# Block attention and an ELU feed-forward on one core: the first stage and the first chunk in a fixed order on all engines

## The chip, the cores and the metric

One core of a Trainium2 chip. A core has five engines that each work through a queue of their own, in order: TensorE (PE in the profile, its weight loads PEld), VectorE (DVE), ScalarE (ACT), GpSimd (POOL) and SyncE (SP), which here only issues DMAs. They wait for each other by semaphores. The time is the device time of one execution in microseconds (us); the profile gives a span, from the first to the last instruction, for one profiled execution.

## The reference

Attention over 4 batches, 8 heads, 768 positions, 64 dimensions, where each query sees its window of 31 neighbours and 24 block summaries (maxima of k, means of v, blocks of 32); its output goes through a feed-forward with an ELU.

```python
k_sum = k.reshape(B, H, nb, block, D).max(axis=3)
v_sum = v.reshape(B, H, nb, block, D).mean(axis=3)
scores_l = scale * np.matmul(q, k.transpose(0, 1, 3, 2))
mask_l = np.abs(pos[:, None] - pos[None, :]) < window
scores_s = scale * np.einsum('bhsd,bhnd->bhsn', q, k_sum) + np.log(block)
scores_all = np.concatenate([np.where(mask_l, scores_l, -1e9), scores_s], axis=-1)
a = np.exp(scores_all - np.max(scores_all, axis=-1, keepdims=True))
a = a / (np.sum(a, axis=-1, keepdims=True) + 1e-09)
attn = np.matmul(a, np.concatenate([v, v_sum], axis=2))
...
h = x @ w_in                       # x: (3072, 512), w_in: (512, 2048)
g = np.where(h > 0.0, h, np.exp(np.minimum(h, 0.0)) - 1.0)
out = g @ w_out                    # w_out: (2048, 512)
```

## The kernel before

Heads go in pairs (`NP` = 4), so that a pair fills 128 partitions. Positions go in thirds of a batch, 256 each, split into four query blocks of 64; a block's keys are the 96 positions around it and the 24 summaries, 120 columns (`KC`). One third of one pair is a *unit*: scores, the lows (`softmax` begins with the negated score's minimum per row, one VectorE instruction per block), four exponentials on ACT with their row sums `z`, a reciprocal on VectorE, a normalization on POOL, four transposes, a copy to `pt`, eight value products, and `take_x`, which splits the output into a rounded high part `xh` (ACT) and a rest `xl` (VectorE).

Two thirds make a *chunk* of 512 tokens; there are six. The feed-forward of a chunk has 16 *slots* `f`: `layer1` is twelve products (high and low parts of x and w) into `h`, then the exponential (ACT, L415), min and max (VectorE, L416 and L417), the high part `gh` (ACT, L420) and the rest `gl` (POOL, L421); `layer2` of the slot before is twelve products into four banks. Between the two stands a piece of unit work: in even slots the scores of a coming unit and the transposes of the current one, in odd slots its value products. In chunk 0 scores, transposes and value products share one bank, `a0`.

The weights come as raw 64-bit words, 32 pieces of 128x512, and each is converted once, in chunk 0 or just ahead of it (`convert`). The steps are called here *mul* (ACT, L96, into the bank `sh`), *lo* (POOL, L98, in place), *sh* and *cv* (VectorE, L100 and L103), *copy* (ACT, L106, the high part) and *sub* (POOL, L107, the rest).

`first_units` does the first two thirds of batch 0 for all four pairs: it loads `kn`, copies its bands and maxima into `k_t`, puts q into block-diagonal tiles `q_t`, sums v by blocks on TensorE (`vsps`), and puts the means into the value tiles. `load_unit` loads q, k and v of a later unit, `summary` the maxima and sums of the next batch.

Order: within `first_units` only SP's queue is written out by hand; in the loop over slots SP's and TensorE's are. All other queues are ordered by a scheduler that goes by costs of its own, led by a few marks (`issue_after`) that hold an instruction until another has been placed. SP's queue has the loads of the first ten weights ahead of the first units' q, k and v; from then on three weights a slot.

Of the kernel before, what the change touches and what calls it, by code (L numbers as in the profile page):

```python
# [26 lines left out]
P = 128  # L27
# [11 lines left out]
def attn_elu_ffn(ctx: ExitStack, tc: tile.TileContext, qT, kT, vT, v, w_in, w_out, out):  # L39
# [32 lines left out]
    raws, weights = {}, {}  # L72

# [12 lines left out]
    def convert(key, turn):  # L86

        raw = raws.pop(key)
        lo_w, hi_w = raw[:, :, 0], raw[:, :, 1]
        sh = psum.tile([P, WC], F32, tag="a1", name="sh")
        bits = sh.bitcast(U32)
        with tc.issue_after(turn[1]):
            nc.scalar.mul(out=sh, in_=hi_w.bitcast(F32), mul=2.0 ** -112)  # L96
        with tc.issue_after(turn[2]):
            nc.gpsimd.tensor_scalar(out=lo_w, in0=lo_w.bitcast(U8)[:, :, 3], scalar1=1 / 32, scalar2=-31 / 64,  # L98
                                    op0=ALU.mult, op1=ALU.add)
        nc.vector.scalar_tensor_tensor(out=bits, in0=bits, scalar=3, in1=lo_w,  # L100
                                       op0=ALU.logical_shift_left, op1=ALU.bitwise_or)
        cv = ffn.tile([P, WC], F32, tag="cv", name="cv", bufs=2)
        nc.vector.scalar_tensor_tensor(out=cv.bitcast(U32), in0=hi_w, scalar=0x80000000, in1=bits,  # L103
                                       op0=ALU.bitwise_and, op1=ALU.bitwise_or)
        w = wts.tile([P, 2, WC], F32R, tag=f"w{key[0]}_{key[1]}", name=f"w{key[0]}_{key[1]}")
        nc.scalar.copy(out=w[:, 0, :], in_=cv)  # L106
        nc.gpsimd.tensor_tensor(out=w[:, 1, :], in0=cv, in1=w[:, 0, :].bitcast(F32), op=ALU.subtract)  # L107
        weights[key] = w
# [4 lines left out]
    def softmax(th, s_ps, sm):  # L113
        mx = att.tile([P, UW, 1], F32, tag="mx", name="mx", bufs=4)
        for t in range(UW):
            w = th * UW + t
            m = mask[:, 0 if w == 0 else 2 if w == NTH * UW - 1 else 1, :]
            low = nc.vector.tensor_tensor_reduce(out=sm[:, t, :], in0=s_ps[:, t, :], in1=m, scale=-scale, scalar=3.0e38,  # L118
                                           op0=ALU.add, op1=ALU.min, accum_out=mx[:, t, :])
        z = att.tile([P, UW, 1], F32, tag="z", name="z", bufs=4)  # L120
        for t in range(UW):
            exp = nc.scalar.activation(out=sm[:, t, :], in_=sm[:, t, :], func=AF.Exp, bias=mx[:, t, :], scale=-1.0,  # L122
                                 accum_out=z[:, t, :])
        nc.vector.tensor_scalar(out=z, in0=z, scalar1=1e-9, scalar2=None, op0=ALU.add)
        nc.vector.reciprocal(out=z, in_=z)
        mul = nc.gpsimd.tensor_tensor(out=sm, in0=sm, in1=z.broadcast_to([P, UW, KC]), op=ALU.mult)  # L126
        return low.ins, exp.ins, mul.ins
# [27 lines left out]
    def put_means(b, p, v_t, copy=None):  # L155
        n = v_t.shape[1]
        src = vs_all[b][KB:KC, p * P:(p + 1) * P].rearrange("n (o d) -> n o d", o=1).broadcast_to([NS, n, P])
# [11 lines left out]
    def first_units():  # L169


        new_x(0)
# [5 lines left out]
        def borrow(shape, name):  # L178
            return wts.tile(shape, F32, tag=free.pop(0), name=name)
# [3 lines left out]
        pt_tags = free[:NP]  # L183
        q_t = [borrow([P, W2, P], f"q{p}") for p in range(NP)]
        sm_tags = free[:NP]
        kn = [borrow([P, E + S], f"kn{p}") for p in range(NP)]
        k_t = [borrow([P, W2, KC], f"k{p}") for p in range(NP)]
        vn = [borrow([P, 2, row], f"vn{j}") for j in range(NTH)]
        mean = borrow([P, 2 * BLK], "mean")
        qn = borrow([P, 2, CH], "qn")  # L190
        sms, pts = {}, {}

        for h in range(2):
# [5 lines left out]
            masked = nc.gpsimd.affine_select(out=m[:, 0:KB], in_=m[:, 0:KB], compare_op=ALU.is_ge, fill=NEG / scale,  # L201
# [17 lines left out]
        for _ in range(2):
            nc.tensor.matmul(idle_ps, zero[:, 0:P], zero, start=True, stop=True)  # L220
        for p in range(NP):
            nc.vector.memset(kn[p][:, 0:E], 0.0)
            for h in range(2 if p < 2 else 0):
                nc.vector.memset(q_t[p][h * D:(h + 1) * D, :, (1 - h) * D:(2 - h) * D], 0.0)

        def load_kn(p):
            nc.sync.dma_start(out=kn[p][:, E:E + S], in_=kT[0, p])

        def load_q(p):
            for h in range(2):  # L230
# [12 lines left out]
        for key in order[:2]:
            load(key)
# [6 lines left out]
        for key in order[2:10]:  # L251
            load(key)

        warm = const.tile([P, 1], F32, name="warm")
        nc.vector.memset(warm, 0.0)
        nc.scalar.activation(out=warm, in_=warm, func=AF.Exp)
        with tc.issue_after(masked.ins):

            per = P // BLK
            nc.gpsimd.memset(mean, 0.0)  # L260
            for r in range(per):
                nc.gpsimd.memset(mean[r * BLK:(r + 1) * BLK, BLK + r:BLK + r + 1], 1.0 / BLK)
            for i in range(2):
                nc.gpsimd.memset(qbd[i], 0.0)
            for p in range(NP):
                nc.gpsimd.memset(kw[p][:, UW - 1, KB - E:KB], 0.0)
                nc.gpsimd.memset(vw[p][QW:KB, UW - 1, :], 0.0)

        ends = []
        for p in range(NP):  # L270
            if p < 2:
                for h in range(2):
                    nc.scalar.copy(out=q_t[p][h * D:(h + 1) * D, :, h * D:(h + 1) * D],
                                   in_=qn[h * D:(h + 1) * D, p].rearrange("d (t q) -> d t q", q=QW))
            band = bass.AP(tensor=kn[p].tensor, offset=kn[p].offset, ap=[list(kn[p].ap[0]), [QW, W2], [1, KB]])
            with tc.issue_after(ends[p - 1][0]) if p > 0 else ExitStack():
                nc.vector.tensor_reduce(out=ks[:, p, :], in_=kn[p][:, E:E + S].rearrange("p (n k) -> p n k", k=BLK),
                                        axis=AX.X, op=ALU.max)
                if p == 0:
                    nc.vector.tensor_copy(out=k_t[p][:, :, 0:KB], in_=band)  # L280
# [262 lines left out]
```

## Time and profile before

| what | value |
|---|---|
| time, median of 3 runs | 677.4 us (676.89 to 679.43) |
| profiled execution: time, span | 677.08 us, 675.3 us |
| mean granted TensorE clock | 0.987 |
| TensorE busy | 651.6 us, 96% of the span |
| VectorE, ScalarE, GpSimd busy | 275.1, 279.9, 248.8 us |
| DMA | 60.21 MB; 28.5% of the engines' time on SP's queue |
| load sizes, KB each | kn 384 (x4), vn 512 (x3), raw weight 512 (x32), v 336 and 40 (x4 each), qn 256 |

Rows of a timeline read: start in us from the span's start, length in us, engine, line, operation, output and inputs by the program's names, sizes, count; in brackets the idle time before it and what ended it. One fp32 product shows as two records, so eight products appear as x16; L412 and L432 use a rounded type with one record each. Rows of a group read: line, engine, operation, sizes, count, then busy us and mean ns of one, then idle time before. In the rows of stretches the columns are start and end, length, busy time (and count) of PE, PEld, DVE, ACT and POOL, granted clock as a share of full speed, mean busy share of the DMA engines, GB/s.

### The profile page before, as it was taken

To read this page: it belongs to the slowest core of one execution; us is meant where nothing else is said; L and a number is where in the kernel's file an instruction comes from. 1 tells how busy PE (TensorE), PEld (TensorE's weight loads), DVE (VectorE), ACT (ScalarE), POOL (GpSimd) and SP (SyncE) were. 2 spreads that over 40 slices of the span, in tenths; PEclk is the share of its full clock that TensorE was granted. 3 is DMA by queue.
4 is the path that set the end of the run, shared out by engine and by line. 5 is a ranking of instruction groups with operands and counts; after the bars stand their busy time and mean duration, and the time that the engine had idled before them with its cause. 6 is when DMAs were issued, how large, how long until landed. Compare 5 with 4: busy or idle time off the path is not lost.

```text
span 675.3 us, 10292 instructions
## 1 busy us (share of the span) xinstructions
PE 651.6 (96%) x3688; PEld 530.0 (78%) x3688; DVE 275.1 (41%) x866; ACT 279.9 (41%) x753; POOL 248.8 (37%) x269
## 2 busy tenths in 40 slices
PE   7879899999999999999999999999999999999996
PEld 4557777888888888888888888888888888888884
DVE  6677986773333543222322553232332222211122
ACT  5465666674333334433433533343443333322221
POOL 7466787983223222322322232222223222222221
PEclk9779999999999999999999999999999999999999
DMA  9969992113112341411212443121312100100001
GB/s 297 298 189 320 323 292 70 35 42 99 47 32 80 98 131 42 125 32 32 61 33 54 139 127 85 38 53 44 94 35 57 32 1 1 63 0 1 0 1 63
DMA packets 88002, 60.21 MB, mean 89 GB/s; under 512 B 48528, under 2 KB 80272, under 8 KB 87952
## 3 DMA queue, kind: packets, MB, share of 16 engines
q1 hardware_dynamic: 84208, 52.74, 28.5%
q10 hardware_dynamic: 3744, 6.82, 2.7%
q8 instruction: 29, 0.48, 0.3%
q14 instruction: 21, 0.17, 0.1%
HBM read 52.46 MB, written 6.29 MB: 87 GB/s over the span
## 4 chain that ended last, share of the span: by engine, by line
PE 84%; DMA 6%; DVE 2%; POOL 2%; SPq 2%; ACT 1%; issue 1%; POOLq 0%; DVEq 0%; ACTq 0%
PE h L412 37%; PE o L432 36%; PE s L386 5%; PE o_ps L139 3%; PE t_ps L132 2%; DMA raw_w<-in_w_out_dram 2%; DMA raw_w<-in_w_in_dram 1%; DMA v<-in_v_dram 1%; DMA n<-in_kT_dram 1%; DMA vw<-in_v_dram 1%; POOL w L107 1%; SPq L158 1%; PE s L289 1%; POOL raw_w L98 1%; POOL gl L421 1%
## 5 line engine op out<-in xcount | busy, mean ns | idle before, releaser
L412 PE MATMUL h<-xh,w 128*128 128x512 f32 x768 | 262.1, 402 | 1.5 <-ACT xh L152 1.5
L421 POOL TENSOR_TENSOR gl<-e,gh 128x512 fp32r<-128x512 f32 x96 | 123.4, 1286 | 206.7 <-issue 114.3
L432 PE MATMUL o<-w,gh 128*128 128x512 f32 x768 | 196.3, 394 | 0.0
L412 PEld LDWEIGHTS h<-xh,w 128*128 128x128 f32 x768 | 144.5, 188 | 33.4 <-ACT xh L152 1.6
L432 PEld LDWEIGHTS o<-w,gh 128*128 128x128 f32 x768 | 141.3, 188 | 27.5 <-ACT gh L420 0.3
L416 DVE TENSOR_SCALAR e<-e 128x512 f32<-128x512 f32 x96 | 49.3, 513 | 260.6 <-ACT e L415 260.5
L412 PE MATMUL h<-xl,w 128*128 128x512 f32 x384 | 150.3, 392 | 0.2 <-DVE xl L153 0.2
L415 ACT ACTIVATE e<-h 128x512 f32<-128x512 f32 x96 | 57.2, 596 | 205.2 <-PE h L412 205.2
L126 POOL TENSOR_TENSOR sm<-sm,z 128x480 f32<-128x480 f32 x48 | 48.1, 1002 | 162.1 <-ACT gh L420 136.7
L432 PE MATMUL o<-w,gl 128*128 128x512 f32 x384 | 105.8, 390 | 0.7 <-POOL gl L421 0.7
L420 ACT CAST gh<-e 128x512 fp32r<-128x512 f32 x96 | 58.9, 614 | 67.4 <-DVE e L417 66.1
L122 ACT ACTIVATE sm<-sm,mx 128x120 f32<-128x120 f32 x192 | 73.6, 384 | 31.2 <-DVE mx L118 28.5
L432 PEld LDWEIGHTS o<-w,gl 128*128 128x128 f32 x384 | 72.1, 188 | 16.2 <-POOL gl L421 1.1
L412 PEld LDWEIGHTS h<-xl,w 128*128 128x128 f32 x384 | 72.5, 189 | 13.3 <-DVE xl L153 0.6
L417 DVE SCALAR_TENSOR_TENSOR e<-h,e 128x512 f32<-128x512 f32 x96 | 66.1, 688 | 1.9
L386 PEld LDWEIGHTS s<-kw,qbd 128*128 128x128 f32 x320 | 42.5, 194 | 5.1 <-DVE xl L153 2.1
L107 POOL TENSOR_TENSOR w<-cv,w 128x512 fp32r<-128x512 f32 x32 | 42.0, 1318 | 11.7 <-ACT w L106 11.1
L386 PE MATMUL s<-kw,qbd 128*128 128x120 f32 x320 | 43.0, 278 | 1.7 <-DVE xl L153 1.7
L118 DVE CUSTOM_DVE_ANT_0 sm<-s,mask 128x120 f32<-128x120 f32 x192 | 42.5, 276 | 4.5 <-PE s L289 3.3
L153 DVE TENSOR_TENSOR xl<-o_ps,xh 128x256 fp32r<-128x256 f32 x48 | 20.0, 421 | 56.8 <-ACT xh L152 56.7
L122 ACT ACTIVATION_READ_ACCUMULATOR sm<-sm,mx 128x1 f32 x192 | 35.9, 187 | 0.0
L133 ACT COPY pt<-t_ps 120x512 f32<-120x512 f32 x44 | 25.6, 583 | 22.8 <-PE t_ps L132 22.4
(65 smaller groups left out, 394.5 us busy)
## 6 DMA issues: line engine op xcount, KB each, us to landing
raw_w<-in_w_in_dram SPq DMA_DIRECT2D x16, 512.0 KB, 6.4
raw_w<-in_w_out_dram SPq DMA_DIRECT2D x16, 512.0 KB, 8.2
out_dram<-ot ACTq DMA_DIRECT2D x24, 256.0 KB, 3.4
qbd<-in_qT_dram SPq DMA_DIRECT2D x80, 64.0 KB, 2.4
kw<-in_kT_dram SPq DMA_DIRECT2D x28, 144.0 KB
vw<-in_v_dram SPq DMA_DIRECT2D x28, 144.0 KB, 3.8
n<-in_kT_dram SPq DMA_DIRECT2D x16, 192.0 KB, 2.6
n<-in_vT_dram SPq DMA_DIRECT2D x16, 192.0 KB, 2.4
```

Source lines behind the costliest of these rows:

```text
L107: nc.gpsimd.tensor_tensor(out=w[:, 1, :], in0=cv, in1=w[:, 0, :].bitcast(F32), op=ALU.subtract)
L118: low = nc.vector.tensor_tensor_reduce(out=sm[:, t, :], in0=s_ps[:, t, :], in1=m, scale=-scale, scalar=3.0e38, op0=ALU.add, op1=ALU.min, a ...
L122: exp = nc.scalar.activation(out=sm[:, t, :], in_=sm[:, t, :], func=AF.Exp, bias=mx[:, t, :], scale=-1.0, accum_out=z[:, t, :])
L126: mul = nc.gpsimd.tensor_tensor(out=sm, in0=sm, in1=z.broadcast_to([P, UW, KC]), op=ALU.mult)
L386: nc.tensor.matmul(s_ps[:, t, :], qbd[u % 2][:, t, :], kw[p][:, t, :], start=True, stop=True)
L412: nc.tensor.matmul(h_ps, w[:, a, cols], bb[:, cc, :], start=(k == 0), stop=(k == 3 * NCC - 1))
L415: exp = nc.scalar.activation(out=e, in_=h_ps, func=AF.Exp)
L416: nc.vector.tensor_scalar(out=e, in0=e, scalar1=1.0, scalar2=-1.0, op0=ALU.min, op1=ALU.add)
L417: elu = nc.vector.scalar_tensor_tensor(out=e, in0=h_ps, scalar=0.0, in1=e, op0=ALU.max, op1=ALU.add)
L420: nc.scalar.copy(out=gh, in_=e)
L421: low = nc.gpsimd.tensor_tensor(out=gl, in0=e, in1=gh.bitcast(F32), op=ALU.subtract)
L432: nc.tensor.matmul(o_acc[c][s], a[:, s * P:(s + 1) * P], w[:, bb, :], start=first and f == 0, stop=last and f == NF - 1)
```

## The change

The whole first stage and the sixteen slots of chunk 0 are written in a fixed order for all five engines; the scheduler keeps VectorE, ScalarE and GpSimd from chunk 1 on. In the first stage scores are formed straight from `kn` and `qn` as loaded, each head by itself on its 64 rows of the array into its 64 partitions of the bank, first all windows (96 columns), then all summaries (24 columns); the tiles `k_t` and `q_t` go. Means for two of the four value tiles are copied from the bank of the sums, not from `vs`. The value sums move on TensorE behind all scores and the first pair's transposes. Weights are loaded and converted in the order (1,0), (1,1), (2,0), (1,2), (2,1) and so on; three are converted ahead of slot 0 and two in each slot, one of them wholly ahead of the slot's exponential. SP loads one weight ahead of v, two behind it, then units and weights by turns.

```diff
+    order = [(1, 0)]
+    for f in range(1, NF):
+        order += [(1, f), (2, f - 1)]
+    order.append((2, NF - 1))
...
-    def convert(key, turn):
+    def convert(tag="a1"):
+        key = todo.pop(0)
...
-        with tc.issue_after(turn[1]):
-            nc.scalar.mul(out=sh, in_=hi_w.bitcast(F32), mul=2.0 ** -112)
-        with tc.issue_after(turn[2]):
-            nc.gpsimd.tensor_scalar(out=lo_w, in0=lo_w.bitcast(U8)[:, :, 3], scalar1=1 / 32, scalar2=-31 / 64,
-                                    op0=ALU.mult, op1=ALU.add)
+        nc.scalar.mul(out=sh, in_=hi_w.bitcast(F32), mul=2.0 ** -112)
+        nc.gpsimd.tensor_scalar(out=lo_w, in0=lo_w.bitcast(U8)[:, :, 3], scalar1=1 / 32, scalar2=-31 / 64,
+                                op0=ALU.mult, op1=ALU.add)
+        yield
         nc.vector.scalar_tensor_tensor(out=bits, in0=bits, scalar=3, in1=lo_w,
                                        op0=ALU.logical_shift_left, op1=ALU.bitwise_or)
...
+        yield
         w = wts.tile([P, 2, WC], F32R, tag=f"w{key[0]}_{key[1]}", name=f"w{key[0]}_{key[1]}")
...
+        def scores(p):
+            q_p = qn[p // 2][:, p % 2]
...
+            for cols in (slice(0, KB), slice(KB, KC)):
+                for th in range(2):
+                    for t in range(UW):
+                        w = th * UW + t
+                        for h in range(2):
+                            rows = slice(h * D, (h + 1) * D)
+                            right = kn[p][rows, w * QW:w * QW + KB] if cols.start == 0 else ks[rows, p, :]
+                            nc.tensor.matmul(banks_of[p, th][rows, t, cols], q_p[rows, w * QW:(w + 1) * QW], right,
+                                             start=True, stop=True)
...
+        put_means(0, 0, v_t[0], act, ps)
+        put_means(0, 1, v_t[1], dve, ps)
+        act(out=vs[KB:KC], in_=ps[KB:KC])
+        one = convert(tag="o3")
+        next(one)
+        put_means(0, 2, v_t[2], pool)
+        put_means(0, 3, v_t[3], pool)
...
+    with tc.manual_schedule(engines=set(engines.values())):
+        first_units()
+        got = {}
+        for n in range(NF):
+            u, odd = divmod(n, 2)
+            h_ps = layer1(0, n)
+            one = convert() if todo else iter(())
+            list(one)
+            if not odd:
+                unit_scores(u + 1, 0)
+                load_unit(u + 2)
...
+            load_more(12 + 3 * (n + 1))
+            e, _ = elu(0, n, h_ps)
+            two = convert() if todo else iter(())
+            next(two, None)
+            split(0, n, e)
+            if not odd:
+                low = unit_low(u + 1)
+                next(two, None)
+                unit_exps(u + 1, low)
+            else:
+                unit_norm(u + 1)
+            list(two)
+            if n > 0:
+                layer2(0, n - 1)
...
+            slot_b(n, 0)
+
+    with tc.manual_schedule(engines={engines["PE"], engines["SP"]}):
+        for n in range(NF, NCH * NF):
```

How the built program's queues read, at three places. GpSimd's queue in chunk 0, from one `gl` to the next (raw_w and w are one weight before and after its conversion, the numbers its slot and the buffer). Before:

```order
L421 TENSOR_TENSOR gl<-e,gh 128x512
L98 TENSOR_SCALAR raw_w_6_690<-raw_w_6_690 128x512
L98 TENSOR_SCALAR raw_w_6_692<-raw_w_6_692 128x512
L107 TENSOR_TENSOR w_5_874<-cv,w_5_874 128x512
L161 COPY kw_75<-ks 128x4x24
L107 TENSOR_TENSOR w_5_883<-cv,w_5_883 128x512
```

GpSimd's queue in slot 2 and the beginning of slot 3, after the change:

```order
L106 TENSOR_SCALAR raw_w_4_203<-raw_w_4_203 128x512
L117 TENSOR_TENSOR w_4_848<-cv,w_4_848 128x512
L106 TENSOR_SCALAR raw_w_3_205<-raw_w_3_205 128x512
L510 TENSOR_TENSOR gl<-e,gh 128x512
L117 TENSOR_TENSOR w_3_897<-cv,w_3_897 128x512
L106 TENSOR_SCALAR raw_w_5_661<-raw_w_5_661 128x512
L117 TENSOR_TENSOR w_5_940<-cv,w_5_940 128x512
```

Before, both lo of the next slot's weights stand ahead of the subs of this slot's; after, each weight's lo and sub follow each other, with the next weight's lo behind them.

ScalarE's queue in chunk 0 over about one and a half slots, before:

```order
L106 CAST w_4_788<-cv 128x512
L96 ACTIVATE sh<-raw_w_5_550 128x512
L420 CAST gh<-e 128x512
L152 CAST xh<-o_ps 128x256
L106 CAST w_5_874<-cv 128x512
L96 ACTIVATE sh<-raw_w_5_552 128x512
L415 ACTIVATE e<-h 128x512
L106 CAST w_5_883<-cv 128x512
L96 ACTIVATE sh<-raw_w_6_690 128x512
L122 ACTIVATE sm,z<-sm,mx 128x120 x4
L420 CAST gh<-e 128x512
```

ScalarE's queue in slot 2 and the beginning of slot 3, after:

```order
L105 ACTIVATE sh<-raw_w_4_203 128x512
L116 CAST w_4_848<-cv 128x512
L501 ACTIVATE e<-h 128x512
L105 ACTIVATE sh<-raw_w_3_205 128x512
L509 CAST gh<-e 128x512
L136 ACTIVATE sm,z<-sm,mx 128x120 x4
L116 CAST w_3_897<-cv 128x512
L149 COPY pt<-t_ps 120x512
L105 ACTIVATE sh<-raw_w_5_661 128x512
L116 CAST w_5_940<-cv 128x512
```

Before, a mul follows right behind the copy of the weight ahead of it, with other work between it and its own copy; after, the first weight's mul and copy are neighbours and the exponential stands behind them.

TensorE's queue in the first stage, from the first scores on (sm, pt and v end in the number of a pair's buffer), before:

```order
L289 MATMUL s<-k_100,q_92 128x120 x8
L289 MATMUL s<-k_101,q_93 128x120 x8
L298 MATMUL vsps<-vn_104,mean 32x512 x2
L298 MATMUL vsps<-vn_105,mean 32x512 x2
L298 MATMUL vsps<-vn_106,mean 32x512 x2
L132 MATMUL t_ps<-ident,sm_219 120x128 x8
L289 MATMUL s<-k_102,q_94 128x120 x8
L132 MATMUL t_ps<-ident,sm_262 120x128 x4
L289 MATMUL s<-k_103,q_95 128x120 x8
```

And after:

```order
L287 MATMUL s<-kn_98,qn_96 64x96 x16
L287 MATMUL s<-ks,qn_96 64x24 x16
L287 MATMUL s<-kn_99,qn_96 64x96 x16
L287 MATMUL s<-ks,qn_96 64x24 x16
L287 MATMUL s<-kn_100,qn_97 64x96 x16
L287 MATMUL s<-ks,qn_97 64x24 x16
L287 MATMUL s<-kn_101,qn_97 64x96 x16
L287 MATMUL s<-ks,qn_97 64x24 x16
L148 MATMUL t_ps<-ident,sm_243 120x128 x8
L309 MATMUL vsps<-vn_92,mean 32x512 x2
```

The value sums stood between the second and the third pair's scores and stand behind all four pairs' and the first transposes now; each pair's eight products of 120 columns are 32 of 96 and 24.

More of the change, by code (lines that the diff above doesn't have):

```diff
@@ L301, in first_units @@
[L301 to L309 removed]
+        load_more(3)
@@ new lines, in vals, with sums @@
+        def vals(p, th):
+            take_x(values(v_t[p], th * UW, pts[p][:, th], ("a0", "o0", "o1", "o2")[2 * (p % 2) + th]), th, p)
+        def sums(j0, j1):
+            for j in range(j0, j1):
+                nc.tensor.matmul(ps[KB:KB + BLK, :], mean[:, BLK - per * j:2 * BLK - per * j],
+                                 vn[j // 2][:, j % 2, :], start=(j == 0), stop=(j == 2 * NTH - 1),
+                                 tile_position=(0, KB))
+        dve, act, pool = nc.vector.tensor_copy, nc.scalar.copy, nc.gpsimd.tensor_copy
@@ new lines, in first_units @@
+        ps = psum.tile([P, row], F32, tag="a1", name="vsps")
+        sums(0, 2 * NTH)
+        norm(3, 0)
+        trans(1, 0, act)
+        trans(1, 1, dve)
+        norm(3, 1)
+        put_means(0, 0, v_t[0], act, ps)
[5 more added lines that the diff above has]
+        put_means(0, 3, v_t[3], pool)
+        trans(2, 0, act)
+        vals(0, 0)
+        trans(2, 1, dve)
@@ L310, in first_units @@
+        vals(0, 1)
+        next(one)
+        trans(3, 0, act)
+        vals(1, 0)
+        trans(3, 1, dve)
+        list(one)
+        vals(1, 1)
+        two = convert()
+        next(two)
+        vals(2, 0)
+        vals(2, 1)
+        next(two)
+        vals(3, 0)
+        vals(3, 1)
         for p in range(NP):
             put_maxima(0, p)
-        return ends[2]
+        unit_scores(0, 0)
+        low = unit_low(0)
+        list(two)
+        three = convert(tag="o3")
+        next(three)
@@ L315, in attn_elu_ffn @@
+        unit_exps(0, low)
+        next(three)
+        unit_norm(0)
+        list(three)
+        for p in range(NP):
+            put_means(0, p, vw[p])
+        load_more(12)
     units = [(third, p) for third in range(2, NTH * B) for p in range(NP)]
@@ L472, in attn_elu_ffn, with slot_b @@
-    convert_more(6, end)
-    first_of = {th // NTH: 4 * (th - 2) for th in range(NTH, NTH * B, NTH)}
-    unit_scores(0, 0)
-    with tc.manual_schedule(engines={mybir.EngineType.PE, mybir.EngineType.SP}):
-        for n in range(NCH * NF):
+    first_of = {th // NTH: 4 * (th - 2) for th in range(NTH, NTH * B, NTH)}
+    def slot_b(n, c):
+        u, odd = divmod(n, 2)
+        if u < len(units):
+            (unit_values if odd else unit_transposes)(u, c)
+        for b, first in first_of.items():
+            if n == 2 * first - 2:
+                means(b, c)
+            p, late = divmod(n - (2 * first - 1), 2)
+            if 0 <= p < NP and not late:
+                put_means(b, p, vw[p])
```

307 lines of the change are left out of this document (150 added, 157 removed).

## The prediction

> **What bounds the kernel now.** I read the page's head, then the busy times of three stretches, and last the timelines of TensorE, ScalarE, VectorE and GpSimd over the first 160 us.
>
> ```profile
> span 675.3 us, 10292 instructions
> ...
> PE 651.6 (96%) x3688; PEld 530.0 (78%) x3688; DVE 275.1 (41%) x866; ACT 279.9 (41%) x753; POOL 248.8 (37%) x269
> ```
> ```profile
> 0.00:45.95 45.95, 34.62 (x233) 25.57 (x233) 31.80 (x124) 25.15 (x88) 29.18 (x64) 0.87 0.95 265
> 45.95:157.95 112.00, 106.04 (x622) 85.33 (x621) 83.58 (x196) 71.66 (x178) 84.82 (x85) 0.99 0.60 176
> 157.95:675.30 517.35, 510.94 (x2840) 419.15 (x2836) 159.69 (x547) 183.12 (x487) 134.83 (x121) 1.00 0.20 55
> ```
> ```profile
> 45.95 0.77 PE L412 MATMUL h<-xh,w 128*128 128x512 f32 x1
> ...
> 54.83 0.48 PE L412 MATMUL h<-xh,w 128*128 128x512 f32 x1
> ...
> 118.69 0.50 PE L412 MATMUL h<-xh,w 128*128 128x512 f32 x1
> ...
> 157.95 0.50 PE L412 MATMUL h<-xh,w 128*128 128x512 f32 x1
> ```
>
> The second fence's columns are stretch, length, and busy time of PE, PEld, DVE, ACT and POOL, then clock, DMA share and GB/s. Three stages show: the first stage until the first layer-1 product (45.95), the sixteen slots of chunk 0 (until 157.95), and the rest, where TensorE idles 6 of 517 us. At the chunk's end six slots take 157.95 - 118.69 = 39.26 us, 13.09 a pair, which is TensorE's own work there; later slots keep that pace, and the change leaves their order as it was. All the change can do lies before 157.95. Sixteen slots at that pace, less one missing layer 2 (12 products of about 0.23, 2.7 us), would take 102; they take 112. So 10 us of stall in chunk 0 and the length of the first stage are what can be won.
>
> **Part 1: one pass of the new slot.** In chunk 0 each slot converts two weights, the first wholly (mul, lo, sh, cv, copy, sub) ahead of the exponential, the second spread behind it. Queues run in order, so the pass closes on itself: ACT's second copy releases POOL's sub, behind that stands the next slot's lo, for which DVE's sh waits, then cv, ACT's copy, behind that the exponential, DVE's min and max, behind them the lows, sh and cv of the second weight, and its copy. Before, POOL did both lo ahead of the subs, and ACT issued the next mul right behind each copy. Its links, from rows:
>
> ```profile
> 57.87 0.60 ACT L415 ACTIVATE e<-h 128x512 f32<-128x512 f32 x1 [1.32 <-PE h L412]
> 60.16 0.62 ACT L420 CAST gh<-e 128x512 fp32r<-128x512 f32 x1 [1.70 <-DVE e L417]
> ...
> 63.77 0.63 ACT L96 ACTIVATE sh<-raw_w 128x512 f32<-128x512 f32 x1
> ...
> 66.02 0.62 ACT L106 CAST w<-cv 128x512 fp32r<-128x512 f32 x1 [1.11 <-DVE cv L103]
> 66.55 0.63 ACT L96 ACTIVATE sh<-raw_w 128x512 f32<-128x512 f32 x1
> ```
> ```profile
> 49.47 0.17 DVE L124 TENSOR_SCALAR z<-z 128x4 f32<-128x4 f32 x1
> 49.67 0.18 DVE L125 RECIPROCAL z<-z 128x4 f32<-128x4 f32 x1
> ...
> 54.22 0.42 DVE L416 TENSOR_SCALAR e<-e 128x512 f32<-128x512 f32 x1
> ...
> 58.50 0.91 DVE L416 TENSOR_SCALAR e<-e 128x512 f32<-128x512 f32 x1 [1.76 <-ACT e L415]
> 59.44 0.69 DVE L417 SCALAR_TENSOR_TENSOR e<-h,e 128x512 f32<-128x512 f32 x1
> ...
> 64.49 0.70 DVE L100 SCALAR_TENSOR_TENSOR sh<-sh,raw_w 128x512 uint32<-128x512 uint32 x1 [1.02 <-ACT sh L96]
> 65.22 0.69 DVE L103 SCALAR_TENSOR_TENSOR cv<-raw_w,sh 128x512 uint32<-128x512 uint32 x1
> ...
> 81.58 0.27 DVE L118 CUSTOM_DVE_ANT_0 sm<-s,mask 128x120 f32<-128x120 f32 x1
> ...
> 82.39 0.68 DVE L417 SCALAR_TENSOR_TENSOR e<-h,e 128x512 f32<-128x512 f32 x1
> 83.00 0.68 DVE L100 SCALAR_TENSOR_TENSOR sh<-sh,raw_w 128x512 uint32<-128x512 uint32 x1
> ```
> ```profile
> 57.84 1.29 POOL L421 TENSOR_TENSOR gl<-e,gh 128x512 fp32r<-128x512 f32 x1
> 59.21 1.44 POOL L98 TENSOR_SCALAR raw_w<-raw_w 128x512 uint32<-128x512 uint8 x2
> 60.87 1.28 POOL L421 TENSOR_TENSOR gl<-e,gh 128x512 fp32r<-128x512 f32 x1 [0.22 <-ACT gh L420]
> ...
> 66.72 1.29 POOL L107 TENSOR_TENSOR w<-cv,w 128x512 fp32r<-128x512 f32 x1 [1.49 <-ACT w L106]
> ```
> ```profile
> L126 POOL TENSOR_TENSOR sm<-sm,z 128x480 f32<-128x480 f32 x13 | 13.5, 1041 | 11.1 <-ACT sm L122 8.0 <-DVE z L125 2.6
> ```
>
> Copy to sub 66.72 - 66.02 = 0.70. Sub to lo 1.37 (GpSimd's 57.84 to 59.21, same size). Lo to sh 0.75 (1.44 for two, back to back about 0.66 each, and 0.09 as from mul's end at 64.40 to 64.49). Sh to cv 0.73, cv to copy 0.80. From the copy on, the exponential starts after 0.53 (66.02 to 66.55) and ends 0.60 later, but min does not take its free 0.42 (54.22, where GpSimd was idle): at 58.50 it ran beside a GpSimd subtraction that ended at 59.13 and itself ended at 59.41, 0.28 later. Here the first weight's sub starts 0.70 after the copy and lasts 1.29, always across min: min ends 0.70 + 1.29 + 0.28 = 2.27 after the copy (1.58 if it never met it, my lower end). Min to the step behind max 0.03 + 0.61 (82.39 to 83.00). Then in an even slot four lows, 0.81 (81.58 to 82.39), in an odd one z and its reciprocal, 0.3. Sh, cv, copy again 1.53. Odd: 0.70 + 1.37 + 0.75 + 1.53 + 2.27 + 0.64 + 0.3 + 1.53 = 9.1. Even: 0.81 instead of 0.3 gives 9.6, and 0.5 more, since the odd slot's gl and the unit's normalization (1.28 and 1.04) stand on POOL ahead of its last sub: 10.1. A pair takes 19.2, where TensorE's work takes 13.1: chunk 0 goes at the pace of the three small engines. TensorE cannot run ahead: the unit's scores and its transposes share one bank, so transposes wait for the lows of their own slot. What TensorE wants from these engines otherwise (gh, gl, xh, weights two slots ahead) is there in time at this pace, and the DMA, at 176 GB/s in this stretch, gets more time than it had.
>
> **Part 2: the first stage.**
>
> ```profile
> 5.01 0.95 DVE L277 TENSOR_REDUCE ks<-kn 128x24 f32<-128x768 f32 x1
> ...
> 43.84 0.62 ACT L106 CAST w<-cv 128x512 fp32r<-128x512 f32 x1 [1.23 <-DVE cv L103]
> ```
> ```profile
> 7.29 3.74 PE L289 MATMUL s<-k,q 128*128 128x120 f32 x16 [2.31 <-DVE k L281]
> ...
> 16.03 5.62 PE L298 MATMUL vsps<-vn,mean 128*32 128x512 f32 x12
> ...
> 22.51 1.94 PE L289 MATMUL s<-k,q 128*128 128x120 f32 x16
> ...
> 36.57 0.69 PE L139 MATMUL o_ps<-pt,v 120*64 120x64 f32 x16 [0.24 <-ACT pt L133]
> ...
> 41.08 1.12 PE L139 MATMUL o_ps<-pt,v 120*64 120x64 f32 x16 [2.80 <-DVE pt L133]
> ```
> ```profile
> L122 ACT ACTIVATE sm<-sm,mx 128x120 f32<-128x120 f32 x52 | 19.9, 383 | 6.3 <-DVE mx L118 3.6 <-issue 2.6
> L133 ACT COPY pt<-t_ps 120x512 f32<-120x512 f32 x8 | 4.6, 572 | 4.9 <-PE t_ps L132 4.9
> L152 ACT CAST xh<-o_ps 128x256 fp32r<-128x256 f32 x12 | 4.3, 367 | 1.1 <-PE o_ps L139 1.1
> L158 DVE COPY v<-vs 24x1024 f32<-24x1024 f32 x2 | 2.1, 1081 | 0.0
> ```
>
> Gone are the copies into k and q tiles, VectorE's four q memsets and the zeroed halves; first scores can start when kn and qn land (about 4.9, as DVE's 5.01). New are 128 quarter products for 32 whole ones: each of 120 columns becomes two of 96 and two of 24, one per head. No row shows a product on half the rows and half the columns of the array. At the pace at 7.29 (3.74/16 = 0.234 a record for 120 columns, two records a product) the first bank needs 16 x 2 records of 96 columns and 8 x 2 of 24: 6.8 in series, 3.4 if both heads run side by side. L139, the nearest row, has its two halves nearly side by side (0.69/16 = 0.043 a record of 64 columns, where 22.51's 1.94/16 = 0.121 for 120 would make it 0.065). I take 3.5: first lows at 8.4, first exponentials at 8.7. Eight groups of four at 4 x 0.38 = 1.5 follow each other on ACT, if DVE's lows and TensorE (whose 5.62 of value sums now stands behind all scores and the first transposes) keep up: last at 21. Then ACT's own list up to the third converted weight: 3 pt copies 1.7, a mean copy 1.1, vs 0.6, three muls 1.7, eight xh 2.9, two copies 1.1, unit 0's exponentials 1.5: 10.6; waits for the value sums 1.7 and, three times, for sh and cv with nothing between, 1.5 each: 6.3. That copy comes at 37.9, against 43.84 for the third copy before. Ends: 6 sooner without these waits, 7 later with scores in series.
>
> The edits in SP's order (kn and qn ahead of vn, the first weight ahead of v, units between weights) and the weights in order of need I cost at nothing: kn, qn, vn, three weights, v and unit 0 are 7.8 MB by the DMA list, in by 29.4 at the stretch's 265 GB/s, and asked for at 32 or later; if they come later, the first product follows one for one. The means taken from PSUM for two pairs spare v the step through vs, a copy of about 0.7 that ACT's list holds either way.
>
> A rule that speaks against this: the Trainium skill, TensorEngine Tiling (Array Packing), "Gotcha 1: PSUM Pressure", says that different row tiles cannot access one PSUM bank at the same time, and both heads write one bank. By it the four sets serialize, the first stage ends 7 later and the time is 715. No run so far shows it.
>
> **The sum.** From the third copy at 37.9, fourteen passes (slots 0 to 13) of 19.2 a pair: 134.4. About 1.0 in slot 6, where ACT evicts the next batch's means ahead of the next mul. From slot 13's second copy to slot 14's lows 0.70 + 0.5 + 1.37 + 0.75 + 1.53 + 2.27 + 0.64 + 0.81 = 8.6, transposes 0.7 (as many columns as the 0.69 at 36.57), slot 15 half a pair, 6.5. Slot 16 starts at 189.1 instead of 157.95: 31 us later, and the rest follows unchanged. The profiled execution took 677.1 beside its span of 675.3 (the median of the runs is 677.4): **708 us**.
>
> Bounds: min never beside sub, 14 x 0.69 = 10 less; first stage 6 sooner; scores in series 7 more; the clock rival's 3 and 0.3 a pass for the links, 4, more. Together 692 to 722.
>
> **Rivals.**
> - *TensorE keeps its pace* (0.08), the other side: if the three engines overlapped neighbouring slots, chunk 0 would take its 102 from a first product at about 34 (37.9 less one copy, mul, four exponentials and a wait): slot 16 at 136, 22 sooner, 655. It decides where a pass is under 6.55. For it: DVE, ACT and POOL are each busy only 72 to 85 of 112 us. Against it: order, not busy time, makes the pass.
> - *The loop is half as bad* (0.07): passes of 7.5 to 8, as when min stays free and links overlap: 14 x 1.8 less than forecast, 676 to 690.
> - *The clock drops in the new gaps* (0.05 for a time beyond my range by it): after 2.80 idle the 16 records at 41.08 took 1.12 instead of 0.69. In even slots TensorE would idle 3.7 before the transposes; at half rate layer 1 ends some 0.4 after the exponential is due, 7 times 0.4, 711. The Trainium skill, TensorE: Matmul & The Clock Gate, "What's actually happening", puts the idle window at about 3.4 us; the 2.80 here was enough.
> - *Nothing moves*: first stage and loop cancel, 674 to 681: 0.03.
>
> **Chances.** Forecast with its bounds 0.77. Half a per cent is about what a measurement of this kernel can tell from no change. Faster 0.08 (the first rival), same 0.04, slower 0.88.
>
> **What would show it.** Right: in chunk 0 layer-1 starts 9 to 10 us apart, POOL's lo directly behind sub, DVE's sh waiting for it, TensorE waiting for DVE at the transposes; the third copy near 37.9; min near 1.0. Wrong: layer-1 starts 6.6 apart there, or exponentials in the first stage with holes of several us, which would put the term on the first stage instead.

## The result, and the profile after

The changed kernel takes 709.67 us (median of 4 runs, 707.47 to 713.68) against 677.14 for the kernel before beside it: 1.0489 times as long, 95% interval 1.0461 to 1.0516. I had forecast 708. The page's head, and TensorE's first layer-1 product of slots 0, 9, 15 and 16 in its timeline:

```profile
span 707.7 us, 10646 instructions
...
PE 659.1 (93%) x3880; PEld 533.0 (75%) x3880; DVE 273.9 (39%) x856; ACT 278.1 (39%) x750; POOL 243.6 (34%) x262
```
```profile
34.19 0.48 PE L495 MATMUL h<-xh,w 128*128 128x512 f32 x1
...
125.63 0.47 PE L495 MATMUL h<-xh,w 128*128 128x512 f32 x1
...
182.96 0.78 PE L495 MATMUL h<-xh,w 128*128 128x512 f32 x1
...
190.61 0.50 PE L495 MATMUL h<-xh,w 128*128 128x512 f32 x1
```

The busy totals of the small engines hardly moved. The first product comes 11.8 sooner (45.95 before), slot 16 comes 32.7 later (157.95 before), and the span is 32.4 longer: all of it lies in chunk 0. From slot 9 to 15 a pair of slots takes (182.96 - 125.63)/3 = 19.1 us; before it was 13.09. The same by stretches (columns as in the prediction):

```profile
0.00:34.19 34.19, 28.23 (x440) 20.00 (x441) 23.81 (x110) 21.33 (x82) 18.73 (x50) 1.00 0.98 274
34.19:190.61 156.42, 119.77 (x607) 93.97 (x606) 88.43 (x200) 73.31 (x181) 88.86 (x91) 0.88 0.48 144
190.61:707.70 517.09, 511.06 (x2840) 419.04 (x2836) 161.65 (x547) 183.43 (x487) 135.97 (x122) 1.00 0.20 55
```

In chunk 0 no engine is busy for more than 120 of 156 us. What they wait for, longest in total first (the view of waits up to 195 us, first stage included: engine and line, for what, sum, times, longest):

```profile
ACT w L116 <- DVE cv L112: 54.1, 23, 3.7
POOL w L117 <- ACT w L116: 40.7, 22, 3.3
DVE sh L109 <- POOL raw_w L106: 31.0, 16, 3.1
DVE e L502 <- ACT e L501: 28.2, 17, 5.8
PE t_ps L148 <- DVE mx L129: 27.7, 8, 7.7
```

The first four are links of the prediction's loop; in the last one TensorE waits for it. One odd pass and the start of an even one, slots 5 and 6, in the timelines of ScalarE, GpSimd and VectorE:

```profile
86.93 0.62 ACT L116 CAST w<-cv 128x512 fp32r<-128x512 f32 x1
91.21 0.62 ACT L116 CAST w<-cv 128x512 fp32r<-128x512 f32 x1 [2.62 <-DVE cv L112]
95.96 0.62 ACT L116 CAST w<-cv 128x512 fp32r<-128x512 f32 x1 [1.10 <-DVE cv L112]
...
105.94 0.62 ACT L116 CAST w<-cv 128x512 fp32r<-128x512 f32 x1
```
```profile
87.62 1.29 POOL L117 TENSOR_TENSOR w<-cv,w 128x512 fp32r<-128x512 f32 x1 [0.92 <-ACT w L116]
89.00 0.65 POOL L106 TENSOR_SCALAR raw_w<-raw_w 128x512 uint32<-128x512 uint8 x1
91.91 1.29 POOL L117 TENSOR_TENSOR w<-cv,w 128x512 fp32r<-128x512 f32 x1 [2.27 <-ACT w L116]
...
97.15 1.27 POOL L117 TENSOR_TENSOR w<-cv,w 128x512 fp32r<-128x512 f32 x1
98.50 0.64 POOL L106 TENSOR_SCALAR raw_w<-raw_w 128x512 uint32<-128x512 uint8 x1
```
```profile
89.68 0.70 DVE L109 SCALAR_TENSOR_TENSOR sh<-sh,raw_w 128x512 uint32<-128x512 uint32 x1 [1.13 <-POOL raw_w L106]
92.36 1.13 DVE L502 TENSOR_SCALAR e<-e 128x512 f32<-128x512 f32 x1 [1.26 <-ACT e L501]
```

ScalarE's second copy of slot 4 is at 86.93, GpSimd's sub at 87.62, the next lo at 89.00, VectorE's sh at 89.68, the first copy at 91.21; min starts at 92.36, beside the sub that began at 91.91, and ends only at 93.49, 0.29 after that sub; the second copy follows at 95.96. Every engine idles while its turn in the ring comes round.

### The profile page after: what moved, and what is told of

It reads as the page before. It is cut to its first block, busy times and chain, and to the rows that moved or that the text cites. A ratio compares the mean times of both kernels' runs of the same rounds, so it can differ in the third digit from the quotient of the medians.

```text
span 707.7 us, 10646 instructions
## 1 busy us (share of the span) xinstructions
PE 659.1 (93%) x3880; PEld 533.0 (75%) x3880; DVE 273.9 (39%) x856; ACT 278.1 (39%) x750; POOL 243.6 (34%) x262
## 4 chain that ended last, share of the span: by engine, by line
PE 76%; DVE 8%; POOL 7%; ACT 6%; issue 1%; DMA 0%; POOLq 0%; ACTq 0%; DVEq 0%
PE h L495 33%; PE o L520 31%; PE s L461 4%; PE o_ps L155 3%; POOL w L117 3%; DVE e L502 2%; PE t_ps L148 2%; ACT w L116 2%; DVE sh L109 2%; DVE cv L112 2%; DVE e L503 2%; POOL raw_w L106 1%; POOL gl L510 1%; PE s L287 1%; ACT gh L509 1%
## 5 line engine op out<-in xcount | busy, mean ns | idle before, releaser
L495 PE MATMUL h<-xh,w 128*128 128x512 f32 x768 | 268.4, 411 | 0.0
L495 PEld LDWEIGHTS h<-xh,w 128*128 128x128 f32 x768 | 149.0, 194 | 33.2 <-issue 0.8
L502 DVE TENSOR_SCALAR e<-e 128x512 f32<-128x512 f32 x96 | 51.6, 538 | 276.6 <-ACT e L501 276.5
L495 PE MATMUL h<-xl,w 128*128 128x512 f32 x384 | 153.6, 400 | 0.0
L495 PEld LDWEIGHTS h<-xl,w 128*128 128x128 f32 x384 | 74.8, 195 | 13.4
L148 PE MATMUL t_ps<-ident,sm 128*120 128x128 f32 x192 | 30.9, 288 | 29.7 <-DVE mx L129 27.7
L148 PEld LDWEIGHTS t_ps<-ident,sm 128*120 128x120 f32 x192 | 23.5, 143 | 38.2 <-issue 20.1
L116 ACT CAST w<-cv 128x512 fp32r<-128x512 f32 x32 | 19.8, 620 | 57.6 <-DVE cv L112 54.1
```

The lines of the kernel that those rows point to most:

```text
L148: nc.tensor.transpose(t_ps[0:KC, t, :], sm[:, t, :], ident)
L495: nc.tensor.matmul(h_ps, w[:, a, cols], bb[:, cc, :], start=(k == 0), stop=(k == 3 * NCC - 1))
L502: nc.vector.tensor_scalar(out=e, in0=e, scalar1=1.0, scalar2=-1.0, op0=ALU.min, op1=ALU.add)
```

## The experiments

Theory: the ring sets the pace, and each link taken out shortens every pass. Rivals: the ring only looks closed and the small engines are simply full or in each other's way; the first stage is at fault; the clock. For the cuts `convert` is divided into five steps, lo | mul | sh, cv | copy | sub, and `steps(g, k)` runs the next k; this alone leaves every queue as in the kernel after.

**Cut one: lo ahead of the sub.**

```diff
-            one = convert() if todo else iter(())
+            one = ahead.pop()
             list(one)
...
+            ahead.append(convert() if todo else iter(()))
+            steps(ahead[0], 1)
             list(two)
```

> The changed kernel with one link cut: GpSimd's lo for the next slot's first weight stands ahead of its last sub in this slot (and likewise ahead of the third weight's sub in the first stage); all else in the same order. The loop theory: sh no longer waits for copy, sub and lo (2.8 to 3.3 us from the second copy) but for ScalarE's pt or xh copy and mul (0.53 + 0.48 or 0.27 + 0.72 = 1.5 to 1.7), so a pair of passes falls from 19.2 to about 16.3 and fourteen passes save 20: about 689. Rival, contention: what costs is that VectorE's min runs beside GpSimd's sub; that stays, so no gain beyond 2: about 708. Rival, the first stage is at fault: unchanged, 709.

Measured 694.32, ratio 1.0257 (1.0242 to 1.0273): 15 us of the 32 are back, against some 20 expected; the contention rival had 2 at most, and min still takes 1.1 beside the sub in most slots here. From slot 9 to 15 a pair takes 16.8 instead of 19.1.

**Cut two: exponential, min and max ahead of the first copy and its sub.**

```diff
-            list(one)
+            steps(one, 3)
...
             e, _ = elu(0, n, h_ps)
+            list(one)
```

> The changed kernel with another link cut: in each slot of chunk 0 the exponential (and VectorE's min and max behind it) is issued ahead of the first weight's copy and sub, not behind them; lo, mul, sh and cv stay where they were. The loop theory: from cv's start min ends after 0.61 + 0.46 instead of 0.80 + 2.27, so 2.0 less a pass, fourteen passes save 28: about 682. Rival, contention: min merely gets free of sub, 0.69 a pass, 10 in all: about 700. Rival, the first stage: 709.

Measured 695.78, ratio 1.0281 (1.0264 to 1.0298): 14 us, half of what was expected and nearer to the 10 of the contention rival, since min now takes its free 0.42 in every slot. But what sets the pace here is a shorter ring. ScalarE's copies from slot 9 on:

```profile
120.20 0.62 ACT L117 CAST w<-cv 128x512 fp32r<-128x512 f32 x1 [1.06 <-DVE cv L113]
...
124.49 0.62 ACT L117 CAST w<-cv 128x512 fp32r<-128x512 f32 x1 [2.13 <-DVE cv L113]
...
128.78 0.62 ACT L117 CAST w<-cv 128x512 fp32r<-128x512 f32 x1 [2.60 <-DVE cv L113]
```

They come 4.29 apart, one weight after the other. By the links of the prediction, copy, sub, the next lo, sh, cv and the next copy are 0.70 + 1.37 + 0.75 + 1.53 = 4.35: the conversion closes on itself even without the exponential. Two such rounds are a pass of 8.6, where the whole ring took 9.0 and 10.0. From slot 9 to 15 a pair of slots takes 17.8.

**Both cuts.**

> Both cuts at once (the next lo ahead of the last sub, and the exponential ahead of the first copy). The loop theory: a pair of passes is 6.3 + 6.0 = 12.2, under TensorE's 13.1, so chunk 0 goes at TensorE's pace from slot 1 on (about 44.5), slot 16 starts near 143 instead of 190.6: about 664, faster than the kernel before (677). If the links add up but TensorE is held by something else (the shared bank a0, cold clock after gaps): 670 to 685. Contention rival: 698 to 700.

Measured 679.68, ratio 1.0046 (1.0031 to 1.0061). The two add up (15 and 14 alone, 30 together), a pair takes 14.9, but it is not the 664 of a chunk at TensorE's pace. The timelines of GpSimd, VectorE and ScalarE in an even slot show what is left of that shorter ring: still one round of it in each slot, 4.30 from the first copy (at 122.05) to the second.

```profile
122.75 1.30 POOL L119 TENSOR_TENSOR w<-cv,w 128x512 fp32r<-128x512 f32 x1 [0.69 <-ACT w L117]
124.13 0.66 POOL L103 TENSOR_SCALAR raw_w<-raw_w 128x512 uint32<-128x512 uint8 x1
```
```profile
124.82 0.70 DVE L110 SCALAR_TENSOR_TENSOR sh<-sh,raw_w 128x512 uint32<-128x512 uint32 x1 [0.95 <-POOL raw_w L103]
```
```profile
126.35 0.62 ACT L117 CAST w<-cv 128x512 fp32r<-128x512 f32 x1 [1.08 <-DVE cv L113]
```

The second weight's lo (124.13) stands behind the first weight's sub, and VectorE waits for it. The shorter ring had been hidden behind the longer one; that is why cut two, and both together, gave less than the links they removed.

**More work on the ring and off it.** Two GpSimd instructions on a scratch tile, once ahead of the first lo in every slot, once behind gl in even slots (`more` issues both):

```diff
+            more()
             one = convert() if todo else iter(())
...
             split(0, n, e)
+            if not odd:
+                more()
```

> The kernel after with two more GpSimd instructions on a scratch tile (128x256 each, in the form of lo, together about 0.7) ahead of the first weight's lo in every slot of chunk 0, that is on the link from the last subtraction to lo. Loop theory: every pass of slots 0 to 13 gets longer by the whole 0.7, 14 x 0.7 = 9.8, 719 to 720. Rival, lo is only near the path and has slack there: less than half, 710 to 714.

> The kernel after with the same two GpSimd instructions behind gl in every even slot, where GpSimd idles about 1.9 us ahead of the last subtraction because ScalarE's copy is not there yet. Loop theory: off the loop, no change, 709 to 711. Rival, GpSimd's load or its sharing with VectorE sets the pace: 8 x 0.7 = 5.6 more, 715.

On the link (the first hunk alone) the time is 724.74, ratio 1.0716 (1.07 to 1.0732); off it (the second alone) 710.43, ratio 1.0504 (1.0481 to 1.0527). GpSimd's timeline, first on the link, then off it:

```profile
83.31 1.26 POOL L119 TENSOR_TENSOR w<-cv,w 128x512 fp32r<-128x512 f32 x1
84.66 0.90 POOL L125 TENSOR_SCALAR junk<-junk 128x256 f32<-128x256 uint8 x2
85.64 0.64 POOL L108 TENSOR_SCALAR raw_w<-raw_w 128x512 uint32<-128x512 uint8 x1
```
```profile
105.21 1.28 POOL L517 TENSOR_TENSOR gl<-e,gh 128x512 fp32r<-128x512 f32 x1 [0.60 <-ACT gh L516]
106.57 0.90 POOL L125 TENSOR_SCALAR junk<-junk 128x256 f32<-128x256 uint8 x2
107.55 1.27 POOL L119 TENSOR_TENSOR w<-cv,w 128x512 fp32r<-128x512 f32 x1
```

The pair of instructions pushes lo back by 85.64 - 84.66 = 0.98, not the 0.7 that I had put down. ScalarE's copies show where it goes: from the third copy to slot 13's second one, fourteen passes, it is 147.7 us (40.08 to 187.79) instead of 134.9, which is 12.8 of the 13.7 that 14 x 0.98 would be. Only the pass that waits for the means hides its share (10.8 instead of 10.6), so the link has next to no slack. Not all of the 15.1 that the time grew by is the link's, though: the third copy itself came 1.3 later (40.08 instead of 38.76), ahead of all added work. The same work in an idle place (GpSimd waits 0.93 there in the kernel after, not the 1.9 I had written) costs 0.8 us in eight slots, within the spread. GpSimd's load as the cause is out: what counts is the place in the queue. Contention is no rival to the ring but a part of it: min takes 1.10 to 1.17 beside the sub in all slots of the kernel after but one, 0.42 in cut two, where no sub runs beside it.

**The first stage: do both heads run side by side?**

```diff
-                    for t in range(UW):
+                    for t2 in range(2 * UW):
+                        h, t = divmod(t2, UW)
                         w = th * UW + t
-                        for h in range(2):
```

> The kernel after, with one change: in the first stage's quarter scores all products of head 0 of a bank come first and then all of head 1, so that neighbours in the queue use the same 64 rows and columns of the array. If both heads of the kernel after run side by side although they write one PSUM bank, 32 records of 96 columns now take about 2.6 to 3 us instead of the 1.53 to 1.56 there (0.043 to 0.049 a record), scores end later and the first exponentials stay near 7.5 while the last come up to 3 later. If writing one bank had already put them in series, nothing changes: 1.5 for 32 records, time within 1 us of 709.7.

TensorE's timeline of the kernel after, then with the heads in turn, then of cut one, whose heads are interleaved as in the kernel after:

```profile
4.99 1.56 PE L287 MATMUL s<-kn,qn 64*64 64x96 f32 x32
...
7.28 1.53 PE L287 MATMUL s<-kn,qn 64*64 64x96 f32 x32
...
9.53 1.53 PE L287 MATMUL s<-kn,qn 64*64 64x96 f32 x32
```
```profile
5.01 2.35 PE L287 MATMUL s<-kn,qn 64*64 64x96 f32 x29
...
8.18 0.29 PE L287 MATMUL s<-kn,qn 64*64 64x96 f32 x1
...
10.78 0.29 PE L287 MATMUL s<-kn,qn 64*64 64x96 f32 x1
```
```profile
4.91 2.75 PE L294 MATMUL s<-kn,qn 64*64 64x96 f32 x32
```

The first records of a run can't decide it: in the same interleaved order they take 1.56 in the kernel after and 2.75 in cut one. Most likely the clock came up at another moment, but the profile's clock column does not show it. The later sets can: the 64 records of one pair take 9.53 - 7.28 = 2.25 interleaved and 10.78 - 8.18 = 2.60 in turn. One after the other, at the 0.121 a record of 120 columns of the kernel before (row at 22.51), 32 records of 96 and 32 of 24 columns would take 32 x 0.121 = 3.9, by estimate. So the two heads do overlap, although both write one PSUM bank, best with neighbours on different quarters of the array and in part even in turn. By the rule "Gotcha 1: PSUM Pressure" of the Trainium skill, TensorEngine Tiling (Array Packing), the order could not have mattered; the 2.25 against 2.60 do not agree with it for this use.

In this run, a single one, the last first-stage exponential comes 1.75 later (21.60 against 19.85) and so does the third copy (40.52 against 38.76), but the time is 709.53. Of the 1.75 part may be the slow first records: in cut one the same exponential comes at 21.11. Slot 16 is at 190.7 nevertheless: slot 15 took 6.3 there, in the kernel after 7.65 at a lower clock (its first product 0.78 instead of 0.48).

**A scheduler in chunk 0 again, with the new first stage fixed.** TensorE and SP stay fixed in the chunk.

```diff
         first_units()
+    with tc.manual_schedule(engines={engines["PE"], engines["SP"]}):
         got = {}
```

> The changed kernel's first stage in its fixed order, but VectorE's, ScalarE's and GpSimd's queues in chunk 0 given back to the scheduler (SP's and TensorE's stay written out). The loop theory: the loss lies in chunk 0's order alone; the third weight's copy comes near 38.8 instead of 43.8 and the sixteen slots take about what they took before (112 from the first product), so slot 16 starts near 148 to 153 and the time is 667 to 673, faster than before. Rival, the first stage is at fault: about 700 or more.

Measured 679.25, ratio 1.0049 (1.0029 to 1.0069), outside the 667 to 673 expected. Slots 0 and 6 take 10.2 and the others 6.2 to 7.6, the chunk 114.6 (the kernel before 112), but the first product comes at 48.61. GpSimd's timeline and TensorE's:

```profile
31.22 0.64 POOL L103 TENSOR_SCALAR raw_w<-raw_w 128x512 uint32<-128x512 uint8 x1 [15.28 <-DMA raw_w<-in_w_in_dram]
```
```profile
37.37 1.11 PE L154 MATMUL t_ps<-ident,sm 128*120 128x128 f32 x4 [15.12 <-POOL sm L149]
```

The scheduler, free in the chunk, put lo of weights that had not landed into GpSimd's queue ahead of normalizations of the first stage; GpSimd stood 15.28 us before one load, 1.60 and 1.51 before the next two, and the transposes stood 15.12 behind them. The chunk's order is about as good as before, but the gain of the first stage is lost to these misplaced waits.

**No lo behind a sub.** Both cuts, and the second weight's lo one slot early as well; then the same in the first stage.

```diff
-            ahead.append(convert() if todo else iter(()))
-            steps(ahead[0], 1)
+            for _ in range(2):
+                ahead.append(convert() if todo else iter(()))
+                steps(ahead[-1], 1)
             list(two)
```
```diff
         put_means(0, 3, v_t[3], pool)
+        two, three = convert(), convert(tag="o3")
+        steps(two, 1)
+        steps(three, 1)
```

> As e3, and the second weight's lo too is issued one slot early, ahead of the last subtraction, so that no lo stands behind a subtraction. Queue theory: in e3 the sixteen slots of chunk 0 still took 126.4 us (34.2 to 160.6) where TensorE needs 102; the chain left was copy1, sub1, lo2, sh2, cv2, copy2, and behind copy2 xh, xl and the next unit's scores. Without the link sub1 to lo2 (0.70 + 1.38 + 0.7 against nothing) that chain is 2 to 2.5 shorter in a slot, TensorE's waits for xl (8.0) and most of the even slots' excess of 1.7 go: slot 16 near 143, time 660 to 664. Rival, the three small engines simply have no more room (they share ports, min beside a subtraction takes 1.13 instead of 0.42): time stays at 676 to 680. Rival, the longer first stage or weights that land late hold it: first product later than 35, waits of GpSimd for a DMA, 668 to 672.

> As e5, and in the first stage the los of the second and third weight are issued right behind the first one's and the two mean copies, ahead of the first weight's subtraction. Queue theory: in e3's first stage ScalarE's list waited for sh and cv of each weight; the los stood behind the subtractions there too (subtraction 30.89, next lo 32.24). About 1 us of the first product's 34.2 goes for the first two, up to 2 for the third, time 0.5 to 2 below e5. Rival, the list is bound by the attention work between (transposes, values): no change against e5 within 0.5. Rival, the weights land too late (in e4 the fourth weight's lo waited for its load until 31.2, later ones until 33.5 and 35.6): GpSimd waits ahead of its first subtraction and it gets 1 to 2 us slower.

Measured 671.27, ratio 0.9911 (0.9887 to 0.9935), and 670.27, 0.9905 (0.9887 to 0.9922), which are not apart from each other. Both beat the kernel before, but not by the 13 to 17 us expected of the first. The second from its first product on:

```profile
33.00:90.50 57.50, 47.85 (x262) 38.03 (x261) 45.15 (x106) 36.33 (x92) 43.50 (x46) 0.94 1.04 323
90.50:151.00 60.50, 60.36 (x348) 48.20 (x347) 40.46 (x94) 37.52 (x89) 44.64 (x46) 1.00 0.30 71
```

From slot 7 on TensorE is busy all the time (60.36 of 60.50 us). The rest of the stall lies in slots 0 to 6, where the DMA share is 1.04 (it sums the time of packets, so it can pass 1). The kernel before shows the same halves:

```profile
45.95:99.30 53.35, 47.39 (x279) 37.45 (x278) 44.08 (x104) 34.52 (x90) 38.95 (x41) 0.99 1.03 313
99.30:157.95 58.65, 58.65 (x345) 47.88 (x344) 39.50 (x93) 37.15 (x89) 45.87 (x45) 1.00 0.21 51
```

**What holds slots 0 to 6?** First the two worst places of the run above: unit 1 loaded ahead of three weights, the block sums behind the slot's last step, and in slot 6 transposes and means ahead of the second copy, the means evicted by VectorE instead of ScalarE. Then, in slot 0, the lows first on VectorE, and on GpSimd the lo of slot 0's two weights ahead of unit 0's normalization.

```diff
         load_unit(0)
+        load_unit(1)
         load_more(6)
-        load_unit(1)
...
+            if n == 6:
+                layer2(0, n - 1)
+                slot_b(n, 0)
             list(two)
```
```diff
+            if n == 0:
+                low = unit_low(1)
             steps(one, 2)
```

> As e6, with the two places mended where its chunk 0 still loses time: unit 1 is loaded ahead of the fourth to sixth weight (in e6 its scores waited 2.61 us for kw in slot 0), the next batch's block sums (VectorE's reductions, one of which waited 1.64 for its load ahead of xl) are issued behind the slot's last step, and in slot 6 transposes and means come ahead of the second weight's copy, the means evicted by VectorE. Theory: what is left in e6 is these two places (slot 0 takes 10.6 and slot 6 10.9, where their neighbours take 6.3 to 7.2). Slot 0 gains 2 to 3, slot 6 2 to 3: 664 to 666. Rival: the three small engines are at their limit all through the chunk and give the time back later: 669 to 671.

> As e8, and in slot 0 alone the next unit's lows come first on VectorE, and the los of the first two weights of slot 0 ahead of unit 0's normalization on GpSimd. In e8 slot 0 still takes 10.6 us although no load is waited for: TensorE's transposes wait 5.96 for the lows, which stand behind sh, cv, min and max, and these behind the lo behind the normalization. Theory: the lows come about 4 earlier, slot 0 takes 6 to 8, and since the conversions have no more to do than before, 2 to 4 of it remain at slot 16: 666 to 668. Rival: in slots 1 to 7 the small engines are at their limit (VectorE has the next batch's block sums there, 8 x 0.95), and what slot 0 gains is given back by slot 8: 669 to 671.

Measured 669.82, ratio 0.991 (0.9891 to 0.993), and 669.72, 0.9895 (0.9878 to 0.9911): nothing and nothing, within the 669 to 671 of both rivals, by which what one slot gains is given back later. In the second slot 0 does shrink from 10.6 to 5.8 us, and slot 2 grows to 12.1; slot 7 comes at 90.7, as at 90.5 and 89.9 in the two before. What TensorE waits for in slot 2, and VectorE shortly before it, by their timelines:

```profile
51.40 1.17 PE L475 MATMUL s<-kw,qbd 128*128 128x120 f32 x8 [2.90 <-DMA kw<-in_kT_dram]
```
```profile
44.50 0.70 DVE L110 SCALAR_TENSOR_TENSOR sh<-sh,raw_w 128x512 uint32<-128x512 uint32 x1 [2.32 <-DMA raw_w<-in_w_in_dram]
```

Loads: TensorE for a unit's keys, VectorE for a weight.

**Two weights a slot instead of three.**

```diff
-            load_more(12 + 3 * (n + 1))
+            load_more(12 + 2 * (n + 1))
```

> As e11, with one number changed: two weights are asked for in a slot of chunk 0 instead of three, so that the weights' loads are spread to slot 10 instead of slot 7. In e11 slot 0 took 5.8 instead of 10.6, but slot 7 came at 90.7 as in e8 (89.9) and e6 (90.5): TensorE waited 2.90 for a unit's kw, VectorE 2.32 for a weight and 3.3 for block sums' inputs, and the DMA share is 1.03 from 33 to 90.7, with 22 weights among its 17.98 MB. DMA theory: the loads set the pace up to slot 7. Seven weights fewer, 3.6 MB at 316 GB/s, are 11 us of transfers; slot 7 then comes when the engines allow, at 82 to 86, and the time is 661 to 665. Rival: VectorE's block sums and the conversions are the limit there, and the waits for loads only fill their gaps: 669 to 671. Rival on the other side: weights now come late for their conversion: over 672.

```profile
33.00:87.80 54.80, 47.57 (x265) 37.65 (x263) 45.28 (x107) 36.38 (x93) 42.87 (x45) 0.97 1.08 326
87.80:148.30 60.50, 60.34 (x348) 48.19 (x347) 41.15 (x95) 36.39 (x88) 45.28 (x46) 1.00 0.32 88
```

Measured 667.8, ratio 0.986 (0.984 to 0.9879). It is the fastest here, 42 us below the kernel after and 9.6 below the kernel before. Slot 7 comes 2.9 sooner, where the DMA theory had 5 to 9, and slot 2 still takes 11.6; the wait for keys is gone, and for the block sums' inputs only 0.9 of waiting is left. But at the place of that wait TensorE now has another, on VectorE:

```profile
51.28 2.06 PE L475 MATMUL s<-kw,qbd 128*128 128x120 f32 x8 [3.05 <-DVE xl L175]
```

The interval just touches that of the run before, so the gain of this one number is likely and not shown. The DMA share stays at 1.08, and VectorE is busy 45 of 55 us there: how much of the 7 us that TensorE still idles before slot 7 is due to loads and how much to VectorE stays open.

## Why the prediction was right, point by point

- **The pass.** Odd 9.1 and even 10.1 were forecast; 86.93 to 95.96 is 9.03, and on to 105.94 is 9.98. The fourteen passes from the third copy (38.76) to slot 13's second one (173.64) take 134.9; 134.4 and 1.0 for the means were forecast. The links agree as well, in slots 5 and 6: copy to sub 0.69 (0.70), sub to lo 1.38 (1.37), lo to sh 0.68 (0.75), min's end 2.28 after the copy (2.27). The extra 0.5 of even passes is there, the odd slot's sub at 97.15 being 1.19 behind its copy.
- **Slot 6** was too small a term: its vs copy waits 2.00 for the means and the pass takes 10.6 instead of 9.1, 1.5 and not 1.0.
- **Min's free time** was read off a wrong row: at 54.22 in the kernel before GpSimd was not idle, a sub ran there until 54.34. The 0.42 holds even so: cut two has it in every slot, with no sub beside it.
- **The first stage** ended as forecast, but by two errors that cancel, which is luck. Scores were costed at 3.4 side by side from the 3.74 at 7.29; that is what 16 such records took at 27.82 with a granted clock of 0.50 (3.77), and not what they took at 22.51 with one of 1.00 (1.94). Here the first two banks were done 2.5 after their start (4.99 to 6.38 + 1.08, row below). That too is a matter of the one execution: in cut one, with the same scores, the first 32 records alone took 2.75 instead of 1.56. First exponentials came at 7.49 instead of 8.7, and the last ended at 20.23 instead of 21. The list from there to the third copy took 18.5 instead of 16.9, all of it waits, and the copy came at 38.76 (37.9 forecast). The bound "7 later with scores in series" stays untested: no run put the scores wholly in series, and the heads in turn cost at most 1.75.

```profile
6.38 1.08 PE L287 MATMUL s<-ks,qn 64*64 64x24 f32 x32
```

- **The tail**, 15.8 from slot 13's second copy to slot 16, took 17.0. Here the clock rival has its share, as the 0.78 at 182.96 shows. In the middle of the chunk it appears too, as in TensorE's rows below, but TensorE is not in the ring there and nothing followed from it:

```profile
47.58 1.08 PE L148 MATMUL t_ps<-ident,sm 128*120 128x128 f32 x4 [7.74 <-DVE mx L129]
...
66.59 1.08 PE L148 MATMUL t_ps<-ident,sm 128*120 128x128 f32 x4 [3.26 <-DVE mx L129]
```

- **SP's order at nothing** was right for this kernel: up to 195 us the only wait for a DMA in the view of waits is VectorE's for kn, 2.2 in all. That the ring, which slowed the chunk to a DMA share of 0.48, made it so is likely and not shown by itself; with the ring gone, loads are among what holds slots 0 to 6.
- **The rival "TensorE keeps its pace", 655,** was the price of the intent, and no version reached it: it left out the stalls of slots 0 to 6, which the kernel before has too (99.30 - 45.95 = 53.4 us for seven slots, where 13.09 a pair, less one missing layer 2, would be 43).

## What to carry to other kernels

Before fixing an order on several in-order queues, follow one instruction's successors from queue to queue until you are back on the first; if the way closes, add up its links, for no pass can be shorter than that sum, however low the busy shares are. Work on which another engine waits (here lo, 0.65 us long) goes ahead of work that itself waits for a late result. When such a ring is cut, expect the next shorter one to decide, and cost that one too before promising the whole difference.

## What the runs showed of the hardware that I had not expected

- Two 64x64 fp32 products on opposite quarters of the array overlap while writing different partitions of one PSUM bank: 64 records (32 of 96 and 32 of 24 columns) in 2.25 us interleaved, 2.60 with the heads in turn, and an estimated 3.9 one after the other.
- A GpSimd tensor_scalar of 128x256 that I had taken as half of lo's 0.65 adds 0.98/2 = 0.49 to its queue. Half the columns cost three quarters here; the two also differ in their output's type (f32 against uint32).
- The length of an idle gap alone did not tell whether the transposes behind it ran at the lower clock. They took 1.08 instead of 0.62 after 3.26 idle in the kernel after, and after 2.38 in the run with more work off the link (at 125.76), but 0.62 after 4.32 in the run with more work on the link (at 70.84).
